# A mixture of experts after attention: a written order for three engines from the first mixture's last two steps on, and a branch put in front of the last stores

## The chip, the cores and the metric

The kernel runs on one core of a Trainium2 chip. The metric is the device time of one launch in microseconds (us), the median of several runs. Each core has five engines that run their own instruction streams in order: TensorE (PE in the rows, with PEld for its weight loads), VectorE (DVE), ScalarE (ACT), GpSimd (POOL) and SyncE (SP). They meet through semaphores only. Here SP issues the loads, and POOL issues the indirect DMAs that scatter rows into a scratch table and the finished rows into the output.

## The reference, cut to what matters

```python
def reference(**kw):                       # q, k, v: 2 x 8 x 768 x 64
    attn = _attn_ref(q, k, v, lam)         # decaying attention, blocks of 64
    x = attn.transpose(0, 2, 1, 3).reshape(1536, 512)
    h = x @ w_in                           # first mixture: 512 -> 2048
    x = (h * np.cos(h)) @ w_out            # 2048 -> 512
    logits = x @ w_gate                    # second mixture: 8 experts
    e_idx = np.argmax(logits, axis=1)
    ...
    for e in range(8):
        mask = e_idx == e
        h = np.maximum(x[mask] @ w1[e], 0.0)      # 512 -> 1024
        out[mask] = gate_w[mask, None] * eom[mask, e, None] * (h @ w2[e])
    return out
```

Each of the 1536 tokens goes to one of eight experts, and its output row is scaled by a softmax weight and a sigmoid of the row itself.

## The kernel before, in words

Matmuls in fp32 precision are made of three fp32r matmuls, with each operand split into a high and a low part: high by high, high by low, low by high. So every weight piece (128 x 1024) is loaded into a `raw` buffer by SP, cast to its high part by ACT and reduced to its low part by DVE; there are five `raw` buffers.

The stages are: attention; the first mixture in steps `B` (256 tokens and a piece of the weights each), whose last three token blocks are finished last (`FIRST`); experts 0 and 1 (`HALVED`) in eight steps `H`, of four tiles of 128 rows in two halves each; experts 2 to 7 in steps `C`, with 208 rows each in two tiles of 104 (`c_first`, `c_second`); then the end.

**The router.** When a block of 256 tokens is finished, `r_tr` transposes it (PE) and copies it to `x2T` (ACT, L582), `r_mm` multiplies by the gates (PE, `lps`, L589), `r_arg` transposes the logits back (PE, `l2ps`, L603) and finds the expert on DVE, and `r_rank` counts the rows of each expert (PE, `rps`, L629 to L632) and scatters the block's rows to the table `xs_d`. After the last block, `routed` issues the loads of the experts' rows from it (`hrows`, L714; `rows`, L736).

**One H step.** `h_l1` multiplies a tile of 128 rows by half of w1 (12 matmuls of 128 x 512 into `hh`, L826) and ACT takes the relu (`hr`, L832). `h_turn` transposes it (4 on PE, `hT`, L838), ACT casts the high part (`hg`, L840) and DVE makes the low part (`hg`, L841). `h_l2` multiplies by half of w2 (12 matmuls into `acc`, L847). `h_prep` and `c_split` transpose rows of x into `xs` (`xps`, L721; ACT L722, DVE L723). `row_scale` works out a row's scale on ACT and DVE (`ng`, L672, first; `who`, L685, last), `finish` scales a tile (`y`, L695 on ACT for the first tile, L697 on DVE for the second) and POOL sends it to the output (L698), one indirect DMA per tile, the "put".

**What orders the work.** Up to step `WHOLE`, the first of experts 2 to 7, the program is written step by step, and the Tile framework's scheduler decides how the instructions follow one another on each engine. From `WHOLE` on, `tc.manual_schedule` fixes PE, DVE and ACT to the written order; SP and POOL are left to the scheduler throughout. After the last step stand a memset of a small tile `warm` on POOL that waits for all puts (L1086), then the load of the count `over` and the branch `tc.If(over > 0)` (L1149). Behind it is a general path for experts that have more rows than their tiles; with these inputs it isn't taken. At last the program's end (L1195), where all engines meet.

```python
    for i in range(NSA + 1, WHOLE):
        step(i)
    phase = tc.manual_schedule(engines={
        mybir.EngineType.PE, mybir.EngineType.DVE, mybir.EngineType.Activation})
    phase.__enter__()
    ends.clear()
    for i in range(WHOLE, len(steps) + LAG):
```

Of the kernel before, what the change touches and what calls it, by code (L numbers as in the profile page):

```python
# [28 lines left out]
def kernel(  # L29
# [130 lines left out]
    order += [(w, e, p) for e in range(HALVED, E) for p in range(EP) for w in ("w1", "w2")]  # L160
# [412 lines left out]
    def r_tr(j):  # L573
# [89 lines left out]
    def row_scale(r, e, n):  # L663
        m = r.shape[0]
        ng = pools["sc"].tile([128, n], F32, tag="ng", name="ng")[0:m]
        ex = pools["sc"].tile([128, n, E], F32, tag="ex", name="ex")[0:m]
        sm = pools["sc"].tile([128, n], F32, tag="sm", name="sm")[0:m]
        ez = pools["sc"].tile([128, n], F32, tag="ez", name="ez")[0:m]
        with ExitStack() as back:
            for ins in ends[-1] if ends else ():  # L670
                back.enter_context(tc.issue_after(ins))
            nc.vector.tensor_scalar(  # L672
                ng.unsqueeze(2), r[:, :, DM + e:DM + e + 1], -1.0, None, ALU.mult)
            for t in range(n):
                nc.scalar.activation(
                    out=ex[:, t, :], in_=r[:, t, DM:DM + E], func=AF.Exp, bias=ng[:, t:t + 1],
                    accum_out=sm[:, t:t + 1])
            nc.scalar.activation(  # L678
                out=ez.unsqueeze(2), in_=r[:, :, DM + E + e:DM + E + e + 1], func=AF.Exp, scale=-1.0)
            nc.vector.tensor_scalar(sm, sm, 1e-9, None, ALU.add)  # L680
# [3 lines left out]
            who = pools["sc"].tile([128, n, 1], I32, tag="who", name="who")[0:m]  # L684
            nc.vector.tensor_copy(out=who, in_=r[:, :, CID:CID + 1].bitcast(I32))  # L685
        return sm, who
# [114 lines left out]

    def c_second(i):
# [12 lines left out]
        if p == EP - 1:  # L815
            acc_t.pop(e)
            s, who = scl.pop(e)
            for z in range(2):
                finish(accs[z], z, s, who[:, z, :])

    def h_l1(e, x, half, turn):
        h = pools["l1"].tile([128, 512], F32, tag="l1", name="hh")
        for z in range(2):
            for kk in range(2):
                for n, (xx, ws) in enumerate(((0, 0), (0, 1), (1, 0))):
                    nc.tensor.matmul(  # L826
                        h, lhsT=x[:, xx, 2 * z + kk, :],
                        rhs=wt["w1", e, 2 * half + z][:, ws, kk * 512:(kk + 1) * 512],
                        start=(z + kk + n == 0), stop=(z == 1 and kk == 1 and n == 2))
            turn()  # L830
        y = tmp_p.tile([128, 512], F32, tag="t", name="hr")
        nc.scalar.activation(out=y, in_=h, func=AF.Relu)  # L832
        return y

    def h_turn(y):
# [6 lines left out]
        return g  # L842

    def h_l2(e, half, g, acc, turn):
        for z in range(4):
            for gs, ws in ((0, 0), (0, 1), (1, 0)):
                nc.tensor.matmul(  # L847
                    acc, lhsT=g[:, gs, z, :], rhs=wB(("w2", e, 2 * half + z // 2), ws, z % 2),
                    start=(half == 0 and z == 0 and gs + ws == 0), stop=(half == 1 and z == 3 and gs == 1))
            if z == 1:  # L850
                turn()
# [9 lines left out]
    def routed():  # L861
# [6 lines left out]
        c_rows(HALVED + 1)  # L868
# [27 lines left out]
    def first(i):  # L896
# [19 lines left out]
        elif ph == "H":  # L916
            y_t[i] = h_l1(j[0], xsp[j], p, turn)
            if j[1] == 1:
                del wt["w1", j[0], 2 * p], wt["w1", j[0], 2 * p + 1]
            if j == (HALVED - 1, 1) and p == 1:  # L920
                for t in range(2):
                    c_split(HALVED, t)
                c_scale(HALVED)

    def second(i):
        ph, j, p = steps[i]
        if p == 0 or (ph == "B" and j < FIRST and p == HP):
            acc_t[j] = [acc_tile([128, DM], "acc") for _ in range(1 if ph == "H" else 2)]
# [18 lines left out]
        elif ph == "H":  # L947
            e, t = j
            h_l2(e, p, g_t.pop(i), accs[0], turn)
            if t == 1:  # L950
                del wt["w2", e, 2 * p], wt["w2", e, 2 * p + 1]
                for _ in range(4 if e == 0 else 0):
                    w_split()
            if p == 1:
                s, who = row_scale(rows.pop(j), e, 1)
                finish(acc_t.pop(j)[0], 0, s, who[:, 0, :])
# [9 lines left out]
    def step(i):  # L966
# [4 lines left out]
        if i == NSB:  # L971
            for _ in range(2):
                second(todo)
                todo += 1
            h_prep(1, 0)
        if i == NSB + 2 * HALVED:
            g_t[i - 1] = h_turn(y_t.pop(i - 1))
            turn()
            h_prep(0, 1)
            for _ in range(2):  # L980
                second(todo)
                todo += 1
                turn()
        if i < len(steps):
            first(i)
        turn()
        if i - 1 in y_t:
            g_t[i - 1] = h_turn(y_t.pop(i - 1))
            turn()
        seconds(max(i - LAG + 1, NSB if i == NSB else 0))  # L990
        if NSB - FIRST * REST <= i < len(steps):
# [4 lines left out]
        if i == NSB + 2 * HALVED:  # L996
            h_prep(1, 1)
# [74 lines left out]
    for i in range(NSA + 1, WHOLE):  # L1072
        step(i)
# [4 lines left out]
    for i in range(WHOLE, len(steps) + LAG):  # L1078
        if i < len(steps):
            c_first(i, i > WHOLE)  # L1080
        if i - 1 in y_t:
            g_t[i - 1] = h_turn(y_t.pop(i - 1))
        (second if i - 2 < WHOLE else c_second)(i - 2)
    phase.__exit__(None, None, None)

    behind(nc.gpsimd.memset(warm, 0.0), puts)  # L1086


    def extra(e, pos):
# [8 lines left out]
        r = pools["rows"].tile([128, 2, ROW], F32, tag="rows", name="xrows")[:, 0:1, :]  # L1098
# [14 lines left out]
        s, _ = row_scale(r, e, 1)  # L1113
# [9 lines left out]
        ps = acc_tile([128, KD, 128], "xps")  # L1123
# [13 lines left out]
        acc = acc_tile([128, DM], "xacc")  # L1137
# [11 lines left out]
    with tc.If(over > 0):  # L1149
# [13 lines left out]
        for e in range(E):  # L1163
# [4 lines left out]
            with tc.For_i(0, n):  # L1168
                extra(e, pos)

# [29 lines left out]
```

## Time and profile before

| | us |
|---|---|
| median of three runs | 532.92 |
| the three runs | 532.25, 532.92, 535.16 |
| the profiled execution, its own time | 535.09 |
| span of its records | 533.3 |
| PE busy in the span | 518.3 (97%) |
| DVE busy | 348.0 (65%) |
| ACT busy | 308.6 (58%) |
| POOL busy | 95.7 (18%) |

The mean granted clock of TensorE in the profiled execution is 0.993 of full speed. The profiled execution is one sample of its own: its time is 2.17 us above the median, and its span begins and ends with the records, 1.8 us short of its time. Busy time of an engine is an average over stages; a stage's own limit is read from what ended the idle time there. A matmul's record includes its way through the pipeline, so records of matmuls that follow one another overlap, and what one costs is the distance between the starts.

### The profile page before, as it was taken

To read this page: it belongs to the slowest core of one execution; us is meant where nothing else is said; L and a number is where in the kernel's file an instruction comes from. 1 tells how busy PE (TensorE), PEld (TensorE's weight loads), DVE (VectorE), ACT (ScalarE), POOL (GpSimd) and SP (SyncE) were. 2 spreads that over 40 slices of the span, in tenths; PEclk is the share of its full clock that TensorE was granted. 3 is DMA by queue.
4 is the path that set the end of the run, shared out by engine and by line. 5 is a ranking of instruction groups with operands and counts; after the bars stand their busy time and mean duration, and the time that the engine had idled before them with its cause. 6 is when DMAs were issued, how large, how long until landed. Compare 5 with 4: busy or idle time off the path is not lost. (4 is left out here: it accounts for less than half of the span.)

```text
span 533.3 us, 9385 instructions
## 1 busy us (share of the span) xinstructions
PE 518.3 (97%) x3644; PEld 454.2 (85%) x3644; DVE 348.0 (65%) x652; ACT 308.6 (58%) x536; POOL 95.7 (18%) x130
## 2 busy tenths in 40 slices
PE   7999999999999999999999999999999999999992
PEld 7889988899898998988888998777888888888881
DVE  5887856887877854454555567932667777777730
ACT  3557655767676765554645576724566656665520
POOL 3455110332222220001021100211010101001011
PEclk9999999999999999999999999999999999999997
DMA  8999941345333392202252256842576778777101
GB/s 201 238 248 266 285 154 41 107 170 198 119 119 119 119 330 77 80 3 80 78 169 97 102 162 199 256 146 92 165 214 209 242 228 247 229 231 215 50 26 36
DMA packets 81939, 84.58 MB, mean 159 GB/s; under 512 B 41468, under 2 KB 61948, under 8 KB 81118
## 3 DMA queue, kind: packets, MB, share of 16 engines
q1 hardware_dynamic: 79646, 77.48, 48.3%
q0 software_dynamic: 2240, 6.42, 3.3%
q8 instruction: 30, 0.49, 0.4%
q14 instruction: 23, 0.19, 0.1%
HBM read 66.70 MB, written 17.65 MB: 158 GB/s over the span
## 5 line engine op out<-in xcount | busy, mean ns | idle before, releaser
L487 PE MATMUL acc<-w_out,g 128*128 128x512 f32 x576 | 140.9, 394 | 0.0
L487 PEld LDWEIGHTS acc<-w_out,g 128*128 128x128 f32 x576 | 104.9, 188 | 22.1 <-issue 1.4
L466 PEld LDWEIGHTS h<-xs,w_in 128*128 128x128 f32 x720 | 88.8, 190 | 2.3 <-DVE a L512 0.5
L466 PE MATMUL h<-xs,w_in 128*128 128x256 f32 x720 | 90.6, 282 | 0.0
L487 PE MATMUL acc<-w_w,g 128*104 128x512 f32 x288 | 70.5, 394 | 0.0
L508 DVE SCALAR_TENSOR_TENSOR a<-a,t 128x512 f32<-128x512 f32 x48 | 36.9, 770 | 44.9 <-ACT a L507 44.9
L487 PEld LDWEIGHTS acc<-w_w,g 128*104 128x104 f32 x288 | 46.7, 168 | 15.4
L476 PE MATMUL hw<-xs,w_w 128*128 128x416 f32 x192 | 59.0, 366 | 0.0
L466 PE MATMUL h<-xback,w_in 128*128 128x256 f32 x432 | 54.9, 282 | 0.0
L466 PEld LDWEIGHTS h<-xback,w_in 128*128 128x128 f32 x432 | 52.8, 189 | 1.4 <-issue 0.8
L506 ACT ACTIVATE t<-h,quarter 128x512 f32<-128x512 f32 x48 | 32.9, 686 | 33.1 <-PE h L466 33.0
L477 PE MATMUL hw<-xs,w_w 128*128 128x208 f32 x192 | 49.3, 257 | 0.0
L772 DVE TENSOR_TENSOR w_w<-raw,w_w 128x1024 fp32r<-128x1024 f32 x40 | 48.6, 1215 | 0.0
L515 ACT CAST g<-a 128x512 fp32r<-128x512 f32 x48 | 29.8, 620 | 30.2 <-DVE a L512 30.2
L512 DVE TENSOR_TENSOR a<-t,h 128x512 f32<-128x512 f32 x48 | 32.9, 685 | 19.6 <-ACT t L511 19.3
L511 ACT ACTIVATE t<-a 128x512 f32<-128x512 f32 x48 | 30.3, 631 | 25.1 <-DVE a L508 25.1
L698 POOL DMA_INDIRECT out_dram<-y,who x16 | 16.4, 1023 | 154.8 <-ACT y L695 122.2
L765 ACT CAST w_w<-raw 128x1024 fp32r<-128x1024 f32 x40 | 42.3, 1057 | 0.0
L516 DVE TENSOR_TENSOR g<-a,g 128x512 fp32r<-128x512 f32 x48 | 33.1, 690 | 12.7 <-ACT g L515 11.9
L783 ACT COPY hsum<-hw 128x208 f32<-128x208 f32 x48 | 15.9, 332 | 41.3 <-PE hw L477 41.3
L477 PEld LDWEIGHTS hw<-xs,w_w 128*128 128x128 f32 x192 | 36.6, 191 | 1.0
L476 PEld LDWEIGHTS hw<-xs,w_w 128*128 128x128 f32 x192 | 36.0, 188 | 1.6
(149 smaller groups left out, 743.0 us busy)
## 6 DMA issues: line engine op xcount, KB each, us to landing
raw<-in_moe_w_dram SPq DMA_DIRECT2D x64, 512.0 KB, 4.4
raw<-in_moe_w_in_dram SPq DMA_DIRECT2D x16, 512.0 KB, 3.8
raw<-in_moe_w_out_dram SPq DMA_DIRECT2D x16, 512.0 KB, 4.4
xs_d<-zrow SPq DMA_DIRECT2D x16, 266.0 KB, 4.4
x_d<-xrow SPq DMA_DIRECT2D x6, 532.0 KB, 3.3
k<-in_k_dram SPq DMA_DIRECT2D x12, 256.0 KB, 3.8
q<-in_q_dram SPq DMA_DIRECT2D x12, 256.0 KB, 5.6
v<-in_v_dram SPq DMA_DIRECT2D x12, 256.0 KB, 5.3
```

Source lines behind the costliest of these rows:

```text
L466: nc.tensor.matmul(h[:, f * n:(f + 1) * n], lhsT=wA(key, ws, kk, f), rhs=x[:, xx, kk, :], start=(z == 0), stop=(z == 3 * KD - 1))
L476: nc.tensor.matmul(h, lhsT=wA(key, 0, kk, f), rhs=x[:, kk], start=(kk == 0), stop=False)
L477: nc.tensor.matmul(h[:, 0, :], lhsT=wA(key, 1, kk, f), rhs=x[:, kk, 0, :], start=False, stop=(kk == KD - 1))
L487: nc.tensor.matmul(accs[t][0:m], lhsT=g[:, gs, f, t * m:(t + 1) * m], rhs=wB(key, ws, f), start=(first and n == 0), stop=(last and n == 5))
L506: head = nc.scalar.activation(out=t, in_=h, func=AF.Identity, bias=quarter, scale=INV2PI / WIDE)
L508: nc.vector.scalar_tensor_tensor(out=a, in0=a, scalar=MAGIC, in1=t, op0=ALU.subtract, op1=ALU.subtract)
L511: nc.scalar.activation(out=t, in_=a, func=AF.Sin, scale=-TWOPI)
L512: nc.vector.tensor_mul(out=a, in0=t, in1=h)
L515: high = nc.scalar.copy(out=g[:, 0].rearrange("p f t -> p (f t)"), in_=a)
L516: low = nc.vector.tensor_sub(out=g[:, 1].rearrange("p f t -> p (f t)"), in0=a, in1=g[:, 0].rearrange("p f t -> p (f t)").bitcast(F32))
L765: nc.scalar.copy(out=t[:, 0, :], in_=r)
L772: nc.vector.tensor_sub(out=t[:, 1, :], in0=r, in1=t[:, 0, :].bitcast(F32))
```

## The change

The manual order now begins with step `NSB`, that is before the last two steps of the first mixture are multiplied by w_out, instead of with `WHOLE`. Between the two, `step`'s loop is replaced by a list that is written out by hand. Within it:

- `h_l1` is called in halves of 6 matmuls, and `h_l2` takes the eight matmuls of the high part of its left operand first and the four of the low part last.
- The casts of the last pieces of experts 0 and 1 are called (`convert_early`) behind the router's steps.
- The scales of the rows (`h_scale`) and the stores (`h_out`) are called apart; `c_scale(2)`, the scale of expert 2's rows, stands behind `h_l2` of the seventh H step.
- `c_rows(3)`, the load of expert 3's rows, is no more in `routed` but behind `h_scale(1, 1)`; expert 2's four pieces of w1 are loaded ahead of its four of w2.

At the end, the memset of `warm` is gone, and `c_store(7)`, the scaling and the two puts of the last expert, stands behind the `If`. The general path takes its working tiles from other pools; it isn't run.

```diff
@@
-    order += [(w, e, p) for e in range(HALVED, E) for p in range(EP) for w in ("w1", "w2")]
+    order += [(w, HALVED, p) for w in ("w1", "w2") for p in range(EP)]
+    order += [(w, e, p) for e in range(HALVED + 1, E) for p in range(EP) for w in ("w1", "w2")]
...
+    def c_store(e, accs):
+        s, who = scl.pop(e)
+        for z in range(2):
+            finish(accs[z], z, s, who[:, z, :])
...
-            for z in range(2):
-                finish(accs[z], z, s, who[:, z, :])
...
+            if e < E - 1:
+                c_store(e, accs)
+            else:
+                acc_t["last"] = accs
...
-        for z in range(4):
-            for gs, ws in ((0, 0), (0, 1), (1, 0)):
...
+        for n, (gs, z, ws) in enumerate([(0, z, ws) for z in range(4) for ws in range(2)] + [(1, z, 0) for z in range(4)]):
...
         h_rows(1)
         c_rows(HALVED)
-        c_rows(HALVED + 1)
...
-            if j == (HALVED - 1, 1) and p == 1:
-                for t in range(2):
-                    c_split(HALVED, t)
-                c_scale(HALVED)
...
-    for i in range(NSA + 1, WHOLE):
+    for i in range(NSA + 1, NSB):
         step(i)
...
+    second(NSB - 2)
+    h_l1(H, 0)
+    second(NSB - 1)
+    rout.clear()
+    h_l1(H, 1)
+    r_tr(last, (0,))
+    r_tr(last, (1,))
+    h_l1(H + 1, 0)
+    h_prep(1, 0)
+    r_mm(last)
+    h_turn(H)
+    h_l1(H + 1, 1)
+    r_arg(last)
+    h_l1(H + 2, 0)
+    r_rank(last)
+    convert_early(1)
+    h_l1(H + 2, 1)
+    h_turn(H + 1)
+    routed()
+    h_l2(H)
+    convert_early(1)
+    h_l1(H + 3, 0)
+    h_l1(H + 3, 1)
+    h_turn(H + 2)
+    convert_early(2 * EP * HALVED)
+    h_scale(0, 0)
+    h_l2(H + 1)
+    h_out(0, 0)
+    h_turn(H + 3)
+    h_l2(H + 2)
+    h_prep(0, 1)
+    h_scale(1, 0)
...
+    h_turn(H + 4)
+    h_scale(0, 1)
+    h_scale(1, 1)
+    c_rows(HALVED + 1)
+    c_split(HALVED, 0)
+    h_l1(H + 6, 0)
+    h_l1(H + 6, 1)
+    h_turn(H + 5)
+    c_split(HALVED, 1)
+    convert(2)
+    h_l2(H + 4)
+    h_l1(H + 7, 0)
+    h_l1(H + 7, 1)
+    h_turn(H + 6)
+    convert(2)
+    h_l2(H + 5)
+    h_out(0, 1)
+    convert(2)
+    c_first(WHOLE, True)
+    h_turn(H + 7)
+    h_l2(H + 6)
+    c_scale(HALVED)
+    c_first(WHOLE + 1, True)
+    h_l2(H + 7)
+    h_out(1, 1)
+    for i in range(WHOLE + 2, len(steps) + LAG):
...
-    behind(nc.gpsimd.memset(warm, 0.0), puts)
...
             with tc.For_i(0, n):
                 extra(e, pos)
+    c_store(E - 1, acc_t["last"])
```

How the rows of three engines move. In these listings a row is a line of the kernel, the operation and its tiles; `w_w_1_2` is piece 2 of expert 1 (its last two numbers apart), and the line numbers of the changed kernel are its own.

ACT, from the last cosine step of the first mixture to the last router block, before:

```order
L511 ACTIVATE t<-a 128x512
L202 CAST w_w_1_2_4084<-raw 128x1024
L515 CAST g<-a 128x512
L722 CAST xs<-xps 128x4x128
L678 ACT_TABLE_LOAD
L678 ACTIVATE ez<-hrows 128x1 x2
L675 ACTIVATE ex,sm<-hrows,ng 128x8 x2
L202 CAST w_w_1_3_4174<-raw 128x1024
L582 COPY x2T<-x2ps 128x512 x2
```

and now:

```order
L512 ACTIVATE t<-a 128x512
L516 CAST g<-a 128x512
L849 ACTIVATE hr<-hh 128x512
L583 COPY x2T<-x2ps 128x4x128 x2
L726 CAST xs<-xps 128x4x128
L857 CAST hg<-hT 128x512
L849 ACTIVATE hr<-hh 128x512
L769 CAST w_w_1_2_4154<-raw 128x1024
```

The casts of pieces 2 and 3 of expert 1, which stood in front of the copies to `x2T`, stand behind them.

DVE, behind the totals of the router, before:

```order
L643 TENSOR_TENSOR si<-sl,ov 128x2
L841 TENSOR_TENSOR hg<-hT,hg 128x512
L858 TENSOR_SCALAR more<-more 128x8
L859 TENSOR_REDUCE most<-more 128x1
L841 TENSOR_TENSOR hg<-hT,hg 128x512
L672 TENSOR_SCALAR ng<-rows 104x2
L672 TENSOR_SCALAR ng<-hrows 128x1
L841 TENSOR_TENSOR hg<-hT,hg 128x512
```

and now:

```order
L887 TENSOR_REDUCE most<-more 128x1
L776 TENSOR_TENSOR w_w_1_3_4210<-raw,w_w_1_3_4210 128x1024
L858 TENSOR_TENSOR hg<-hT,hg 128x512
L677 TENSOR_SCALAR ng<-hrows 128x1
L685 TENSOR_SCALAR sm<-sm 128x1
L686 TENSOR_SCALAR ez<-ez 128x1
L687 TENSOR_TENSOR sm<-sm,ez 128x1
L688 RECIPROCAL sm<-sm 128x1
L689 COPY who<-hrows 128x1
L858 TENSOR_TENSOR hg<-hT,hg 128x512
```

The first step of expert 2's scale (`ng` from `rows`, 104x2) stood in front of an `hg`; it is no more in this stretch.

SP, from the loads of the experts' rows on, before:

```order
L714 DMA hrows<-xs_d 128x532 x2
L736 DMA rows<-xs_d 104x2x532
L184 DMA raw<-in_moe_w_dram 128x4x256
L184 DMA raw<-in_moe_w_dram 128x2x512
L184 DMA raw<-in_moe_w_dram 128x4x256 x2
L184 DMA raw<-in_moe_w_dram 128x2x512
L736 DMA rows<-xs_d 104x2x532
```

and now:

```order
L718 DMA hrows<-xs_d 128x532 x2
L740 DMA rows<-xs_d 104x2x532
L185 DMA raw<-in_moe_w_dram 128x2x512
L740 DMA rows<-xs_d 104x2x532
L185 DMA raw<-in_moe_w_dram 128x2x512 x3
L185 DMA raw<-in_moe_w_dram 128x4x256
```

The second load of `rows` (expert 3's) stands behind one load of a weight piece instead of five.

## Rows read from the trace of the kernel before

**Rows 1.** Busy time by stretch: from, to, length; busy us of PE, PEld, DVE, ACT, POOL.

```profile
339.00:404.00 65.00, 62.95 (x335) 51.85 (x333) 33.77 (x88) 34.16 (x67) 8.68 (x8) 1.00 0.54 169
```

**Rows 2.** Timeline at the last router block, PE and ACT: start, us, what, [idle before].

```profile
344.89 1.18 PE L826 MATMUL hh<-w_w,xs 128*128 128x512 f32 x4
346.63 0.64 PE L589 MATMUL lps<-x2T,wgs 128*32 128x256 f32 x8 [0.55 <-ACT x2T L582]
...
344.56 1.05 ACT L202 CAST w_w<-raw 128x1024 fp32r<-128x1024 f32 x1 [1.23 <-DMA raw<-in_moe_w_dram]
```

**Rows 3.** Timeline of PE and DVE in the second layer of experts 0 and 1.

```profile
363.74 0.71 PE L847 MATMUL acc<-w_w,hg 128*128 128x512 f32 x2
365.64 5.28 PE L847 MATMUL acc<-w_w,hg 128*128 128x512 f32 x22 [1.19 <-DVE hg L841]
...
364.77 0.17 DVE L672 TENSOR_SCALAR ng<-rows 104x2 f32<-104x2 f32 x1 [8.91 <-DMA rows<-xs_d]
```

**Rows 4.** Timeline of PE and SP's queue where expert 2 begins.

```profile
389.82 0.35 PE L476 MATMUL hw<-xs,w_w 128*128 128x416 f32 x1
...
392.69 0.55 PE L721 MATMUL xps<-ident,rows 104*128 104x104 f32 x4 [0.30 <-DMA rows<-xs_d]
...
386.82 0.34 SPq L736 DMA_DIRECT2D rows<-xs_d  x1
```

**Rows 5.** Timeline of PE at the last block's logits and ranks.

```profile
348.00 0.38 PE L603 MATMUL l2ps<-ident,lt 128*128 128x128 f32 x2
...
350.30 0.18 PE L629 MATMUL rps<-ohb,upper 128*128 128x8 bf16 x1
```

**Rows 6.** Timeline of the last 18 us, all engines.

```profile
515.43 8.46 PE L487 MATMUL acc<-w_w,g 128*104 128x512 f32 x36
...
521.21 0.69 ACT L695 ACTIVATE y<-acc,sm 104x512 f32<-104x512 f32 x1 [4.26 <-PE acc L487]
522.19 0.99 POOL L698 DMA_INDIRECT out_dram<-y,who  x1 [12.06 <-ACT y L695]
523.93 0.75 DVE L697 TENSOR_SCALAR y<-acc,sm 104x512 f32<-104x512 f32 x1 [6.36 <-PE acc L487]
524.98 1.00 POOL L698 DMA_INDIRECT out_dram<-y,who  x1 [1.79 <-DVE y L697]
529.94 0.10 POOL L1086 MEMSET warm<- 128x1 f32 x1 [3.96 <-DMA out_dram<-y,who]
```

**Rows 7.** The branch's line: sequencer operations, ns min/median/max, first to last start.

```profile
L1149 POOLq EVENT_SEMAPHORE  x6: 17/30/43, 528.3 to 528.7; - x6
...
L1149 ACTq EVENT_SEMAPHORE  x2: 17/17/17, 524.3 to 524.4; - x2
L1149 DVEq EVENT_SEMAPHORE  x2: 21/21/21, 527.9 to 528.0; - x2
...
L1149 ACTq COMPARE_BRANCH  x1: 50/50/50, 521.8 to 521.8; - x1
L1149 DVEq COMPARE_BRANCH  x1: 72/72/72, 524.6 to 524.6; - x1
L1149 POOLq COMPARE_BRANCH  x1: 53/53/53, 525.3 to 525.3; - x1
```

**Rows 8.** The line of the program's end, the same columns.

```profile
L1195 SPq EVENT_SEMAPHORE  x14: 17/28/28, 529.5 to 533.2; - x14
...
L1195 POOLq DRAIN  x3: 40/113/2488, 529.9 to 533.0; - x3
L1195 SPq DRAIN  x3: 7/7/7, 530.2 to 532.7; - x3
```

**Rows 9.** DMA issues from 520 to 533: count, median us to landing.

```profile
out_dram<-y,who POOLq DMA_INDIRECT x2, 3.4
```

**Rows 10.** A weight piece's way from the page; ACT's casts where expert 2 begins.

```profile
raw<-in_moe_w_dram SPq DMA_DIRECT2D x64, 512.0 KB, 4.4
...
387.92 3.15 ACT L202 CAST w_w<-raw 128x1024 fp32r<-128x1024 f32 x3
```

More of the change, by code (lines that the diff above doesn't have):

```diff
@@ L577, in r_tr @@
         x2T = lps_t["x2T"]
-        for t in range(2):
+        for t in tiles:
             ps = acc_tile([128, KD, 128], "x2ps")
@@ L816, in c_second, with h_l1, h_turn @@
             acc_t.pop(e)
-            s, who = scl.pop(e)
-            for z in range(2):
-                finish(accs[z], z, s, who[:, z, :])
[L821 to L835, printed above, removed]
+            if e < E - 1:
+                c_store(e, accs)
+            else:
+                acc_t["last"] = accs
+    hh_t = {}
+    def h_l1(i, z):
+        _, (e, t), half = steps[i]
+        x = xsp[e, t]
+        if z == 0:
+            hh_t[i] = pools["l1"].tile([128, 512], F32, tag="l1", name="hh")
+        h = hh_t[i]
+        for kk in range(2):
+            for n, (xx, ws) in enumerate(((0, 0), (0, 1), (1, 0))):
+                nc.tensor.matmul(
+                    h, lhsT=x[:, xx, 2 * z + kk, :],
+                    rhs=wt["w1", e, 2 * half + z][:, ws, kk * 512:(kk + 1) * 512],
+                    start=(z + kk + n == 0), stop=(z == 1 and kk == 1 and n == 2))
+        if t == 1:
+            del wt["w1", e, 2 * half + z]
+        if z == 1:
+            y_t[i] = tmp_p.tile([128, 512], F32, tag="t", name="hr")
+            nc.scalar.activation(out=y_t[i], in_=hh_t.pop(i), func=AF.Relu)
+    def h_turn(i):
+        y = y_t.pop(i)
         ps = acc_tile([128, 4, 128], "hT")
@@ L841, in h_turn, with h_l2, h_scale, h_out @@
         nc.vector.tensor_sub(out=g[:, 1], in0=ps, in1=g[:, 0].bitcast(F32))
-        return g
-    def h_l2(e, half, g, acc, turn):
-        for z in range(4):
-            for gs, ws in ((0, 0), (0, 1), (1, 0)):
[L847 to L851, printed above, removed]
+        g_t[i] = g
+    def h_l2(i):
+        _, (e, t), half = steps[i]
+        g = g_t.pop(i)
+        if half == 0:
+            acc_t[e, t] = acc_tile([128, DM], "acc")
+        acc = acc_t[e, t]
+        for n, (gs, z, ws) in enumerate([(0, z, ws) for z in range(4) for ws in range(2)] + [(1, z, 0) for z in range(4)]):
+            nc.tensor.matmul(
+                acc, lhsT=g[:, gs, z, :], rhs=wB(("w2", e, 2 * half + z // 2), ws, z % 2),
+                start=(half == 0 and n == 0), stop=(half == 1 and n == 11))
+        if t == 1:
+            del wt["w2", e, 2 * half], wt["w2", e, 2 * half + 1]
+    def h_scale(e, t):
+        scl[e, t] = row_scale(rows.pop((e, t)), e, 1)
+    def h_out(e, t):
+        s, who = scl.pop((e, t))
+        finish(acc_t.pop((e, t)), 0, s, who[:, 0, :])
     def totals():
@@ L946, in second @@
                 del wt["out", p]
[L947 to L956, printed above, removed]
     todo = 0
@@ L970, in step @@
             h_prep(0, 0)
[L971 to L985, printed above, removed]
-        turn()
[L987 to L991, printed above, removed]
+        first(i)
+        turn()
+        seconds(i - LAG + 1)
+        if NSB - FIRST * REST <= i:
             n = 0
@@ L1077, with convert, convert_early @@
     ends.clear()
-    for i in range(WHOLE, len(steps) + LAG):
+    heads.clear()
+    assert not rout and todo == NSB - 2
+    H, last = NSB, FIRST - 1
+    def convert(n=1):
+        for _ in range(n):
+            c_high()
+            c_low()
+    def convert_early(n):
+        for _ in range(n):
+            if nxt["split"] < wide + 2 * EP * HALVED:
+                convert()
+    second(NSB - 2)
[30 more added lines that the diff above has]
+    h_scale(1, 0)
+    h_l2(H + 3)
+    h_out(1, 0)
+    h_l1(H + 4, 0)
+    h_l1(H + 4, 1)
+    h_prep(1, 1)
+    h_l1(H + 5, 0)
+    h_l1(H + 5, 1)
+    h_turn(H + 4)
[24 more added lines that the diff above has]
+    for i in range(WHOLE + 2, len(steps) + LAG):
         if i < len(steps):
[L1080 to L1083, printed above, removed]
+            c_first(i, True)
+        c_second(i - 2)
     phase.__exit__(None, None, None)
-    behind(nc.gpsimd.memset(warm, 0.0), puts)
     def extra(e, pos):
@@ L1097, in extra @@
         who = pools["xt1"].tile([128, 1], I32, tag="who", name="who")
-        r = pools["rows"].tile([128, 2, ROW], F32, tag="rows", name="xrows")[:, 0:1, :]
+        r = pools["rows"].tile([128, 2, ROW], F32, tag="rows", name="xrows")
+        r, spare = r[:, 0:1, :], r[:, 1, :]
         nc.gpsimd.indirect_dma_start(
```

31 lines of the change are left out of this document (13 added, 18 removed).

## The prediction, made before the changed kernel was run

> **What bounds the kernel now.** First the page's busy times, in the table above: PE is busy for 97% of the span, and the change removes no matmul, so only the time in which PE stands still, and what follows its last matmul, can be gained. Then busy time by stretch: from 339 to 404 us, which holds most of the stages that get the written order, PE is busy 62.95 of 65.00 us [rows 1]. So 2.05 us of idle time is all that those records show. Third, the timelines, for what ended each pause; there are three, of 0.55, 1.19 and 0.30 us, 2.04 together [rows 2 to 4]. Since records of matmuls overlap, I price a pause by the distance between starts, less what the work in it costs. Matmuls of 128x512 that wait for nothing cost 0.235 us each (36 in 8.46 [rows 6]), or 0.24 (22 in 5.28 [rows 3]). Last, the end: PE's last matmul ends at 515.43 + 8.46 = 523.89 [rows 6], and the span ends at 533.3. So 9.4 us lie behind the bound, in which only ACT, DVE, POOL, DMA and the branch work.
>
> **The pause in front of the last router block.** PE starts four matmuls at 344.89 and the router's `lps` at 346.63: 1.74 us for four times 0.238, so 0.79 lost. The row puts it down to ACT's `x2T`; ACT itself had stood 1.23 us for a weight piece's DMA, cast it at 344.56 for 1.05, and only then copied `x2T` [rows 2]. In the changed order that cast stands behind the copies, and PE has six matmuls and four transposes between x2T's transposes and `lps`. Two copies have that long. I take all 0.79 as gained. The piece that is cast later is of w2 of expert 1, used only in the second layer, which PE reached at 363 to 371 [rows 3].
>
> **The pause in front of expert 1's second layer.** Two matmuls start at 363.74, the next 22 at 365.64: 1.90 less 0.47, so 1.43 lost to DVE's `hg`. DVE had stood 8.91 us for expert 2's rows and began `ng` of them at 364.77, one place ahead of that `hg` [rows 3]. With `c_scale(2)` moved behind the seventh H step's second layer, nothing in DVE's stretch waits for that DMA; the scale that now stands there reads `hrows`, block 0's rows, which came long before. All 1.43 are gained.
>
> **The pause where expert 2 begins.** From 389.82 to 392.69 are 2.87 us in which PE does 16 matmuls that cost 2.40 by the starts of their eight pairs (0.30 a pair). So 0.47 are lost to the rows of expert 2 or 3, whose load was issued at 386.82 behind five weight pieces [rows 4]. Now it stands behind one piece and waits for its buffer, which `h_scale(1, 1)` gives back, by my placing of that step between 381 and 385. That is 2 to 6 us earlier, against 0.47 lost. All of it is gained: 0.79 + 1.43 + 0.47 = 2.69 for the three, where idle records alone give 2.04.
>
> **What the new order adds.** Between `l2ps` and `rps`, DVE finds the experts of the last block. The two start 2.30 us apart, under nine matmuls of 0.238 and l2ps's own 0.14, which fill it [rows 5]. The list puts only one `h_l1` call of six there: 1.43 + 0.14 = 1.57. So PE may wait 2.30 - 1.57 = 0.73 us. What that chain of DVE steps needs by itself is not shown, since PE was in time; it is between nothing and 2.30, and I take the upper end, because `rps` followed its matmuls without a gap to spare. The count of rows (`cps`) now waits for the last DVE addition of the rank step, which I set at one small DVE step, 0.14 (by the 0.17 of `ng` [rows 3], mostly covered by the matmuls ahead). Together 0.87. The order of terms within `h_l2` changes no count; it gives DVE's low part eight matmuls, 1.9 us, more time. That is cover and no gain of its own. The stage thus gains 2.69 - 0.87 = **1.82**, at most 2.69.
>
> **The end.** Behind the last matmuls ACT scales one tile at 521.21, DVE the other at 523.93, and POOL issues the last put from 524.98 to 525.98 [rows 6]. Then the three branch: ACT at 521.8 with its next row at 524.3, DVE at 524.6 with 527.9, POOL at 525.3 with 528.3, so 2.5, 3.3 and 3.0 us [rows 7]. After that POOL's memset begins at 529.94, and the row puts its wait down to the puts [rows 6]. But the last put lands some 3.4 us after its issue [rows 9], at 528.4, so the memset stood for POOL's own way through the branch. The end is entered at 529.5 by SP and 529.9 by POOL, whose DRAIN takes 2.49, to 532.4; then 0.9 to the end of the span [rows 8].
>
> With the branch in front of the last tiles, ACT takes it behind its last `g`, with 4.26 us of idle time ahead of its `y`, DVE with 6.36 [rows 6]: both cover the 2.5 and 3.3. POOL takes it after expert 6's puts, ahead of 12.06 us of idle time [rows 6]. PE takes it after its last matmul, as now. So the way through the branch is hidden, and the memset's 0.10 goes. POOL's DRAIN can begin at 525.98 and ends at 528.5, about when the put lands. Then SP's walk over its semaphores, 529.5 to 530.2, so 0.7, and the 0.9 of the close [rows 8]: 528.4 + 0.7 + 0.9 = 530.0 against 533.3. The gain is **3.3**. Its bounds: 3.9, if only the DRAIN stands in the way (528.5 + 0.9 = 529.4), and 1.5, if the DRAIN begins when the put has landed (rival one).
>
> The price of the branch decides here, and the rows show it as 2.5 to 3.3 us on each engine [rows 7]. The Trainium skill, "Runtime: NRT & Kernel Launch", section "Instruction fetch mechanics", says that a taken branch whose target lies outside the fetched window makes the engine fetch it before it goes on; the trace agrees with a wait of that kind, and by that rule the jump to the program's end could be a second one (rival three).
>
> **The sum.** 1.82 + 3.3 = 5.1 us. Against the profiled execution that is 535.09 - 5.1 = 530.0. That execution is 2.17 above the median of the runs shown, which are 2.9 apart, so I take the sum off the median: 532.92 - 5.1 = **527.8**. A measurement of this kernel can tell about 0.5%, 2.7 us, from no change, which puts the bound for faster at 530.3.
>
> **Rivals.**
> One: the DRAIN on POOL begins only after the last put has landed, as it did before (529.9, when all was landed). Then 528.4 + 2.49 + 0.9 = 531.8, a gain at the end of 1.5, in all 3.3: **529.6**. For it: DRAIN's 2.49 in the only case shown, and that nothing tells what it waits for. Against it: it took that long with no transfer left. Chance 0.12.
>
> Two: the order only moves the pauses. What PE waits for is late again elsewhere (the rank chain at its full length, a cast that now stands in front of a relu), and the H stretch gains nothing: 532.92 - 3.3 = **529.6**. For it: idle time is only 3% of that stretch [rows 1], and ACT and DVE are each busy over half of it, so an order without pauses is tight. Against it: each of the three waits is for one instruction that the listings show moved. Chance 0.08.
>
> Three: the way through the branch comes back at another jump, on POOL between the last put and the end: 525.98 + 3.0, then the DRAIN's 2.49 and 0.9 make 532.4, a gain of 0.9; in all 2.7, so **530.2**. For it: the code of the end lies behind the general path, and POOL jumps to it. Against it: the present kernel has such a jump behind the memset, and the DRAIN begins in the same tenth of a microsecond as the memset [rows 6, 8]. Chance 0.06.
>
> Four, to the slow side: SP's queue. The load of expert 3's rows now stands in front of seven weight pieces, and until `h_scale(1, 1)` has freed its buffer nothing passes it. The sixth piece of expert 2 lands 4.4 us after its issue [rows 10], so at 385.8 to 389.8 if the rows are issued at 381 to 385. ACT's third cast in the present run begins at about 390.0 [rows 10], which is where the new list has the sixth piece. The margin is 0 to 4 us, and PE has work beyond it for about 5 (a second layer of 12 matmuls, 2.86, and an expert's first layer, 2.40). In a written order ACT stands at that cast with a relu and an `hg` behind it, and PE stops. It decides from some 7 us of delay on. At 10 us PE loses 3 if that cover holds and 10 if it doesn't, with the H stretch's gain gone: 532.92 - 3.3 + 3 = 532.6 to 539.6, in the middle **536.1**. For it: the order of SP's queue, which had sent five pieces ahead of that load and now sends one. Against it: the buffer is freed by steps that PE's own progress brings. Chance 0.04.
>
> **How the numbers follow.** 0.70 is left for the forecast. It holds 526.3 (2.69 + 3.9 gained) to about 529; rivals one to three lie at 529.6 to 530.2, and runs of one kernel scatter by one or two us. The range 526.0 to 530.8 takes them in and leaves out rival four and some scatter. Faster by over 0.5%: the forecast, one and two, 0.90, less 0.07 for measured times that fall beyond 530.3, so 0.83. Within: three and that scatter, 0.13. Slower: rival four, 0.04.
>
> **What would show it.** In the profile of the changed kernel: no pause of PE in front of `lps`, at expert 1's second layer, or in front of expert 2's `xps`; a new one of up to 0.73 in front of `rps`; PE busy for all but about 1 us of the same 65. At the end: the branch's rows on ACT, DVE and POOL ahead of their last tile's rows, POOL's DRAIN right behind the last put, and about 6 us from PE's last matmul to the end of the span instead of 9.4. It is wrong if those 6 stay above 8 (three), if the DRAIN starts after the landing (one), if PE's idle time in the stretch stays at 2 (two), or if PE stops where expert 2 begins (four).

## The result, and the profile after

| | before | after |
|---|---|---|
| median of six runs, us | 534.43 | 528.96 |
| lowest and highest | 532.25, 535.74 | 528.00, 529.86 |
| ratio, 95% interval | | 0.9906 [0.9888, 0.9923] |
| the profiled execution | 535.09 | 529.07 |
| its span | 533.3 | 527.3 |

The change makes the kernel 5.0 us faster by the ratio (0.0094 x 534.43; 4.1 to 6.0 by its interval). The forecast was a sum of 5.1 and a time of 527.8 in a range of 526.0 to 530.8. The sum is what was measured; the time came out 1.2 higher because the kernel before has a median of 534.43 in six runs, 1.5 above that of the three that the forecast started from.

The span on the page of the kernel after, and then busy time in the stretch of [rows 1]:

```profile
span 527.3 us, 9379 instructions
```

```profile
339.00:404.00 65.00, 64.75 (x346) 53.93 (x346) 36.51 (x91) 36.30 (x71) 7.86 (x8) 1.00 0.55 176
```

PE now idles 0.25 us of those 65 instead of 2.05. All of it is one pause, ahead of the ranks. PE's timeline from x2T's transposes to the ranks, after:

```profile
344.00 1.04 PE L582 MATMUL x2ps<-ident,xrow 128*128 128x128 f32 x8
344.79 1.64 PE L841 MATMUL hh<-w_w,xs 128*128 128x512 f32 x6
346.27 0.60 PE L725 MATMUL xps<-ident,hrows 128*128 128x128 f32 x4
346.80 0.64 PE L590 MATMUL lps<-x2T,wgs 128*32 128x256 f32 x8
347.37 0.66 PE L855 MATMUL hT<-ident,hr 128*128 128x128 f32 x4
347.78 1.64 PE L841 MATMUL hh<-w_w,xs 128*128 128x512 f32 x6
349.25 0.38 PE L604 MATMUL l2ps<-ident,lt 128*128 128x128 f32 x2
349.39 1.62 PE L841 MATMUL hh<-w_w,xs 128*128 128x512 f32 x6
351.26 0.18 PE L630 MATMUL rps<-ohb,upper 128*128 128x8 bf16 x1 [0.25 <-DVE ohb L619]
```

`lps` follows without a bracket, where [rows 2] had 0.55. From `l2ps` to `rps` are 2.01 us for matmuls that cost 1.57, so PE loses 0.44 there (0.25 by the records). The 2.01 are the length of DVE's chain, and the trace before has it too: there `l2ps` starts at 348.00 [rows 5], and the chain's last step, which `rps` reads, ends at 349.95, 1.95 later:

```profile
349.78 0.17 DVE L618 CAST ohb<-oh 128x16 bf16<-128x16 f32 x1
```

The end, after: the timeline, the branch's line and the line of the program's end.

```profile
518.43 0.69 ACT L699 ACTIVATE y<-acc,sm 104x512 f32<-104x512 f32 x1 [4.26 <-PE acc L488]
519.42 1.00 POOL L702 DMA_INDIRECT out_dram<-y,who  x1 [12.06 <-ACT y L699]
521.16 0.75 DVE L701 TENSOR_SCALAR y<-acc,sm 104x512 f32<-104x512 f32 x1 [6.36 <-PE acc L488]
522.20 1.00 POOL L702 DMA_INDIRECT out_dram<-y,who  x1 [1.78 <-DVE y L701]
```

```profile
L1214 POOLq EVENT_SEMAPHORE  x6: 17/30/43, 509.5 to 509.9; - x6
L1214 ACTq EVENT_SEMAPHORE  x2: 17/17/17, 516.6 to 516.7; - x2
L1214 DVEq EVENT_SEMAPHORE  x2: 21/21/21, 517.7 to 517.8; - x2
...
L1214 POOLq COMPARE_BRANCH  x1: 53/53/53, 506.7 to 506.7; - x1
...
L1214 ACTq COMPARE_BRANCH  x1: 50/50/50, 514.2 to 514.2; - x1
L1214 DVEq COMPARE_BRANCH  x1: 72/72/72, 514.8 to 514.8; - x1
```

```profile
L1261 SPq EVENT_SEMAPHORE  x14: 17/28/14610, 510.7 to 527.2; - x14
...
L1261 POOLq DRAIN  x3: 40/113/4506, 522.0 to 527.0; - x3
L1261 SPq DRAIN  x3: 7/7/7, 526.0 to 526.7; - x3
```

The way through the branch is about as long as it was (POOL 506.7 to 509.5, ACT 514.2 to 516.6, DVE 514.8 to 517.7, against [rows 7]), but each engine has passed it before its last tile comes. The last put now starts at 522.20 and ends at 523.20, and the span ends 4.1 us later; before, it ended at 525.98, 7.3 us ahead of the end [rows 6].

**Where the time went.** Four starts in PE's timeline cut an execution into stages: the first w_in matmul of the first mixture, its last one, the first w2 matmul of expert 2, and the last matmul of all. Between the second and the third lies the written order; behind the fourth, the end. In each trace, in us (variants without a ratio were run once):

| kernel | to first w_in | w_in | written order | experts 2 to 7 | end | ratio to before |
|---|---|---|---|---|---|---|
| before | 37.88 | 295.17 | 71.11 | 119.34 | 9.76 | |
| after | 37.36 | 295.19 | 68.79 | 119.37 | 6.59 | 0.9906 |
| tail_only | 36.40 | 295.31 | 71.07 | 119.34 | 6.60 | 0.9935 |
| order_only | 37.95 | 295.35 | 68.69 | 119.37 | 9.81 | 0.9972 |
| no_memset | 36.93 | 295.18 | 71.07 | 119.34 | 9.28 | 0.9997 |
| memset_back | 36.47 | 295.28 | 69.08 | 119.37 | 7.94 | 0.9936 |
| cast_front | 36.30 | 295.30 | 68.76 | 119.37 | 6.55 | |
| scale_front | 37.23 | 295.17 | 70.42 | 119.37 | 6.57 | |
| l2_terms | 37.85 | 295.36 | 68.68 | 119.37 | 6.58 | |
| rows_late | 36.28 | 295.23 | 74.24 | 119.37 | 6.59 | |
| b_scale | 36.50 | 295.22 | 69.22 | 119.34 | 9.89 | |
| scale_l2 | 37.05 | 295.24 | 73.80 | 119.37 | 6.59 | |
| best | 37.36 | 295.14 | 68.52 | 119.37 | 6.82 | 0.9895 |
| rank_cover | 36.84 | 295.14 | 68.69 | 119.37 | 6.54 | 0.9903 |

The spans differ by 6.0 us: 2.32 in the written order, 3.17 at the end, and 0.52 ahead of the first w_in matmul, in attention, which the change doesn't touch. That first stage spreads over 1.7 us between executions, the others agree within 0.2 where the program is the same (the written order of `memset_back`, with a pause of 0.19 of its own, within 0.4). So a stage's own length tells tenths where whole times tell whole microseconds.

### The profile page after: what moved, and what is told of

It is laid out like the page before. It is cut to its first block, busy times and chain, and to the rows that moved or that the text cites. A ratio compares the mean times of both kernels' runs of the same rounds, so it can differ in the third digit from the quotient of the medians.

```text
span 527.3 us, 9379 instructions
## 1 busy us (share of the span) xinstructions
PE 517.1 (98%) x3644; PEld 454.7 (86%) x3644; DVE 348.2 (66%) x652; ACT 308.7 (59%) x536; POOL 93.9 (18%) x129
## 5 line engine op out<-in xcount | busy, mean ns | idle before, releaser
L776 DVE TENSOR_TENSOR w_w<-raw,w_w 128x1024 fp32r<-128x1024 f32 x50 | 60.6, 1216 | 0.8 <-ACT w_w L769 0.8
L769 ACT CAST w_w<-raw 128x1024 fp32r<-128x1024 f32 x50 | 52.5, 1056 | 0.0
```

The lines of the kernel that those rows point to most:

```text
L769: nc.scalar.copy(out=t[:, 0, :], in_=r)
L776: nc.vector.tensor_sub(out=t[:, 1, :], in0=r, in1=t[:, 0, :].bitcast(F32))
```

## Experiments

### The two parts apart

The kernel before with the new end (`tail_only`), and the changed kernel with the old one (`order_only`):

```diff
@@ tail_only, in the kernel before
+            if e < E - 1:
+                c_store(e, accs)
+            else:
+                acc_t["last"] = accs
...
-    behind(nc.gpsimd.memset(warm, 0.0), puts)
...
+    c_store(E - 1, acc_t["last"])
@@ order_only, in the changed kernel
-            if e < E - 1:
-                c_store(e, accs)
-            else:
-                acc_t["last"] = accs
+            c_store(e, accs)
...
+    behind(nc.gpsimd.memset(warm, 0.0), puts)
...
-    c_store(E - 1, acc_t["last"])
```

> The kernel before with the new end alone (branch in front of the last tiles, no memset); the order of the stages ahead is as it was. Theory (the two parts add up, and the end is worth what it showed in the changed kernel): PE's pauses of 0.55, 1.19 and 0.30 us stay, and from PE's last matmul to the end of the span there are 6.2 us instead of 9.4, so 3.2 us less, ratio 0.994. Rival (the end only gains beside the new order): under 1 us.

> The changed kernel with the old end (the last tiles' stores and the memset in front of the branch). Theory: PE's last matmul comes 2.7 us earlier than in the kernel before, 9.4 us follow it as before, ratio 0.995. Rival (what the order gains is given back at the end): under 1 us.

`tail_only`: 530.01 against 533.68, ratio 0.9935 [0.9915, 0.9954], which is 2.5 to 4.5 us; by stage 3.16, with the three old pauses by the records (0.41, 1.08, 0.57). `order_only`: 532.14, ratio 0.9972 [0.9961, 0.9984], 0.9 to 2.1 us; by stage 2.42. The end's gain needs no new order, and the order's gain isn't given back at the end. The two ratios add up to 5.0 us, the whole. Why the times of `order_only` show 1.5 us (0.0028 x 533.68) where its stage shows 2.4 isn't settled; the first stage, which each trace samples once, is the only other one that varies.

### What held the end: the branch or the wait for the puts

```diff
@@ no_memset, in the kernel before
-    behind(nc.gpsimd.memset(warm, 0.0), puts)
@@ memset_back, in the changed kernel
     c_store(E - 1, acc_t["last"])
+    behind(nc.gpsimd.memset(warm, 0.0), puts)
```

> The kernel before without the memset that waits for all puts, the branch where it was. Theory (POOL's way through the branch, not the wait for the puts, held the end): from PE's last matmul to the end of the span 9.0 to 9.4 us, so 0 to 0.4 us less, ratio 0.999 to 1. Rival (the memset's 3.96 us of waiting are the cost): 2.5 to 3.3 us less, ratio 0.995.

> The changed kernel with the memset, which waits for all puts, put back at its very end. It tells what POOL's last DRAIN waits for. Theory (the DRAIN takes about 2.5 us by itself, and is partly hidden under the last put's way): landing at 3.4 us after the put's issue, 0.1 for the memset, 2.5 for the DRAIN, 0.8 to close, so 7.9 us from PE's last matmul to the end instead of 6.2, 1.7 us more than the changed kernel, ratio to before 0.994. Rival (the DRAIN waits for the landing anyway, and is short behind it): 0 to 0.3 us more than the changed kernel.

`no_memset`: ratio 0.9997 [0.9982, 1.0013], the end 9.28 instead of 9.76. The memset's 3.96 us of waiting [rows 6] cost at most half a microsecond: POOL was in the branch meanwhile. `memset_back`: 530.03, ratio 0.9936 [0.9921, 0.9952], the end 1.35 us longer than after. POOL's last two rows in its trace, and the DRAIN of the program's end:

```profile
521.69 1.00 POOL L702 DMA_INDIRECT out_dram<-y,who  x1 [1.78 <-DVE y L701]
524.81 0.10 POOL L1236 MEMSET warm<- 128x1 f32 x1 [2.12 <-DMA out_dram<-y,who]
```

```profile
L1262 POOLq DRAIN  x3: 40/113/2498, 524.8 to 527.9; - x3
```

The put has landed 3.1 us after its start, and a DRAIN that starts behind the landing still takes 2.50. So the landing isn't what its time is spent on. In the changed kernel its record starts at 522.0, ahead of the put, and ends at 526.5, 3.3 us after the put's end, while SP's walk, which had waited 14.6 us from 510.7 for the landing at 525.3, is through at 526.0. The DRAIN is the last link, by half a microsecond. Rival one of the prediction would have had the end of `memset_back`.

### One thing of the order, in the kernel before

```diff
@@ b_scale: expert 2's scale behind the last hg called ahead of it, on DVE
-                c_scale(HALVED)
+                with tc.issue_after(g_t["low"].ins):
+                    c_scale(HALVED)
```

> The kernel before with one thing of the change alone: the scale of expert 2's rows is queued on DVE behind the last hg that is called ahead of it, so no hg stands behind the wait for those rows. The stretch from the first mixture's last w_in matmul to expert 2's first w2 matmul is 71.11 us in the kernel before and 71.07 in two others with its order. Theory (the three pauses are not three independent terms: the one at lps was covered by the one at hg, which ended when the rows landed; with that one gone the one at lps counts): the pause at expert 1's second layer is gone, the stretch is 69.3 to 69.8 us. Second theory (three independent terms): 1.43 less, 69.7, with pauses at lps and expert 2's xps as before; the two are told apart by a run in which the pause at lps is short. Rival (what is gained comes back whole at the next wait): 70.8 or more.

The stretch is 69.22, 1.89 less, by this one step. PE in `b_scale`, at `lps`, in the second layer of expert 1 and where expert 2 begins, and the load of expert 3's rows:

```profile
345.22 0.64 PE L589 MATMUL lps<-x2T,wgs 128*32 128x256 f32 x8 [0.47 <-ACT x2T L582]
```

```profile
362.32 3.90 PE L847 MATMUL acc<-w_w,hg 128*128 128x512 f32 x16
```

```profile
383.02 0.88 PE L721 MATMUL xps<-ident,rows 104*128 104x104 f32 x8
...
389.47 0.55 PE L721 MATMUL xps<-ident,rows 104*128 104x104 f32 x4
```

```profile
383.93 0.34 SPq L736 DMA_DIRECT2D rows<-xs_d  x1
```

The pause ahead of `hg` is gone, the one at `lps` stays, and the one at expert 2's `xps` has gone as well, by landing: PE needed those rows 5.5 us after their issue and had them. In the kernel before they took 5.9 (392.69 - 386.82 [rows 4]) and in `tail_only` 6.1; why they were faster in this one execution isn't shown. Neither theory held whole, as the stretch is below the 69.3 of the first and the 69.7 of the second. What was measured is two of the prediction's terms: 71.11 - 1.43 - 0.47 = 69.21.

The first theory needs the pause at `lps` to be covered by the one at `hg`. The execution of `no_memset` seems to say so: it has no pause at `lps`, the same 71.07, and at `hg`

```profile
364.75 5.28 PE L847 MATMUL acc<-w_w,hg 128*128 128x512 f32 x22 [1.72 <-DVE hg L841]
```

1.72 where [rows 3] has 1.19. But the loads of expert 2's rows went out earlier there too, counted from the start of the written order by 0.48 us, as much as `lps` came earlier. What took longer was the load. Its issue before, and its issue and first reading in `no_memset`:

```profile
359.61 0.45 SPq L736 DMA_DIRECT2D rows<-xs_d  x1
```

```profile
358.19 0.45 SPq L736 DMA_DIRECT2D rows<-xs_d  x1
```

```profile
363.88 0.17 DVE L672 TENSOR_SCALAR ng<-rows 104x2 f32<-104x2 f32 x1 [9.43 <-DMA rows<-xs_d]
```

That is 5.16 us before (364.77 [rows 3]), 5.69 in `no_memset` and 5.61 in `tail_only` (363.16 - 357.55), with the same order up to there. A load that differs by half a microsecond between executions can hide a pause of that size, so these traces don't tell whether the pause at `lps` was worth something by itself. No run takes it away alone.

**The buffer, not the queue.** In the kernel before, expert 3's rows are issued 0.2 us after the eight transposes of expert 2's rows end, which are 0.72 long by the starts: 383.02 + 0.72 = 383.74 and 383.93 here, 385.91 + 0.72 = 386.63 and 386.82 in the trace before ([rows 4]; the transposes' row is the first below). There are two such buffers. The other one, with the rows of the second tiles, was read until 402.4 before, and until 378.9 after:

```profile
385.91 0.88 PE L721 MATMUL xps<-ident,rows 104*128 104x104 f32 x8
```

```profile
L685 DVE COPY who<-hrows x2: 133/144/154, 374.6 to 402.4; 128x1 int32<-128x1 int32 x2
```

```profile
L689 DVE COPY who<-hrows x4: 134/134/135, 362.5 to 378.9; 128x1 int32<-128x1 int32 x4
```

```profile
379.19 0.32 SPq L740 DMA_DIRECT2D rows<-xs_d  x1
```

So it is `h_scale(1, 1)`, now some 23 us earlier, that lets the load go.

### Taking single steps back in the changed kernel

```diff
@@ cast_front
+    c_high()
     r_tr(last, (0,))
...
     r_rank(last)
-    convert_early(1)
+    c_low()
@@ scale_front
     h_out(0, 0)
+    nc.vector.tensor_scalar(warm[0:HL, :], rows[HALVED, 2][:, 0, DM + HALVED:DM + HALVED + 1], -1.0, None, ALU.mult)
     h_turn(H + 3)
@@ l2_terms (scale_l2 has this and scale_front)
-        for n, (gs, z, ws) in enumerate([(0, z, ws) for z in range(4) for ws in range(2)] + [(1, z, 0) for z in range(4)]):
+        for n, (gs, z, ws) in enumerate([(gs, z, ws) for z in range(4) for gs, ws in ((0, 0), (0, 1), (1, 0))]):
@@ rows_late
-    c_rows(HALVED + 1)
     c_split(HALVED, 0)
...
     c_split(HALVED, 1)
     convert(2)
+    with tc.issue_after(raw_t["load"].ins):
+        c_rows(HALVED + 1)
```

> The changed kernel with one cast (the high part of piece 2 of expert 1's w2, on ACT) put back in front of the copies to x2T; its low part on DVE stays where it is. Read from the trace: PE's distance from x2T's transposes to lps, 2.80 us in the changed kernel, and the pause ahead of lps, 0 there. Theory (ACT is in order, so the copies wait for the cast, and that for its piece): 0.1 to 0.4 us of pause if the piece has landed when ACT comes to it, since six matmuls and four transposes now stand in between and give about 1 us, and one for one more for each us that the piece lands later. Rival (the cover alone cured this pause): none.

No pause at `lps`, and 68.76. ACT and PE in `cast_front`:

```profile
343.73 1.03 ACT L769 CAST w_w<-raw 128x1024 fp32r<-128x1024 f32 x1
344.66 1.07 ACT L583 COPY x2T<-x2ps 128x512 f32<-128x512 f32 x2
```

```profile
345.82 0.64 PE L590 MATMUL lps<-x2T,wgs 128*32 128x256 f32 x8
```

The cast stands in front of the copies again, but its piece is there, and the copies end at 345.7, just in time for `lps`. So the six matmuls and four transposes in between suffice to cover a cast of 1.03 us, as the rival said. But the run puts back the cast of piece 2. The one that stood directly in front of the copies in the kernel before was piece 3's, and it had first stood 1.23 us for its DMA [rows 2]. Here the copies end 0.1 us ahead of `lps`, so a wait of that kind would hardly have been covered; no run tries it.

> The changed kernel with one small DVE step that reads expert 2's rows (one column of them, into a spare tile) put in front of the low part of hg of the fourth H step. Theory (DVE stands at that step until the rows have landed, some 5.2 us after their issue at 362.3, and hg, queued behind, is late): DVE waits to about 367.4, hg's low part comes at about 368.2, and PE, which needs it after eight of the twelve matmuls that start at 365.65, so at 367.55, pauses 0.5 to 1.0 us. Rival (the pause before was the term order of h_l2, not the DVE step): no pause.

> The small DVE step that reads expert 2's rows in front of hg, as in scale_front, and the old order of terms in h_l2. Theory (the term order is cover: hg's low part is needed after two matmuls instead of eight, six times 0.238 earlier): the pause of 1.46 us grows to 2.9, and the stretch from 70.42 to 71.8. Rival (the term order covers nothing): 1.5 us of pause as before.

In `scale_front` DVE stood 5.78 us, the rows landed 6.3 us after their issue at 361.86, where I had expected 5.2, and PE paused 1.46. DVE and PE there, and PE in `scale_l2`:

```profile
368.15 0.15 DVE L1110 TENSOR_SCALAR warm<-rows 104x1 f32<-104x1 f32 x1 [5.78 <-DMA rows<-xs_d]
```

```profile
368.95 1.20 PE L868 MATMUL acc<-w_w,hg 128*128 128x512 f32 x4 [1.46 <-DVE hg L858]
```

```profile
369.21 3.88 PE L868 MATMUL acc<-w_w,hg 128*128 128x512 f32 x10 [3.24 <-DVE hg L858]
```

One DVE step that reads late rows in front of `hg` brings the pause back, so that mechanism is shown. With the old term order the pause is 3.24 (2.9 expected, and the rows came 0.35 us later in this run), so the cover of six matmuls is worth about their own time, 1.4 us. The stretch grew by more than the pause did, 3.38 against 1.78; see the last section.

> The changed kernel with the old order of terms in h_l2 (the low part of the left operand as every third matmul, so first needed after two matmuls instead of eight). Theory (cover and no gain of its own: DVE's low part is ready before its matmuls start): the stretch from the first mixture's last w_in matmul to expert 2's first w2 matmul within 0.3 us of the changed kernel's 68.80. Rival (the terms' order is what took the pause ahead of expert 1's second layer away): 1 to 1.5 us more, with a pause put down to DVE's hg.

68.68, and no pause but the one at `rps`: the term order alone is cover and no gain, as forecast.

> The changed kernel with the load of expert 3's rows queued on SP behind three more weight pieces (four instead of one). Theory (the rows take 5.9 us from issue to PE, as they did before, and SP's queue sets the issue): issued at about 388 instead of 379.2, so PE's transposes of expert 3's rows, at 389.9 in the changed kernel, stand 3 to 5 us. Rival (the pause before was the rows' own way or DMA load, not their place in the queue): under 1 us.

SP's load and PE's transposes in `rows_late`:

```profile
387.22 0.38 SPq L740 DMA_DIRECT2D rows<-xs_d  x1
```

```profile
392.71 0.58 PE L725 MATMUL xps<-ident,rows 104*128 104x104 f32 x4 [3.76 <-DMA rows<-xs_d]
```

Behind three more pieces the rows go out 9.1 us later, counted from the start of the written order in each trace, PE stands 3.76 us, and the stretch is 74.24. So the queue's order does count once the buffer is early.

### Towards a faster one

```diff
@@ rank_cover and best, with h_turn cut into its transposes and its copies
+    h_turn_pe(H + 1)
     r_rank(last)
...
     h_turn(H + 1)
@@ best alone, for the very last tile
+            nc.scalar.activation(out=y[:, 0:256], in_=acc[:, 0:256], func=AF.Copy, scale=s[:, t:t + 1])
+            nc.vector.tensor_scalar(y[:, 256:DM], acc[:, 256:DM], s[:, t:t + 1], None, ALU.mult)
```

> The changed kernel with two additions: the four transposes of the second H step stand between l2ps and rps on PE (their copies on ACT and DVE stay where they were), and the very last tile is scaled in two halves by ACT and DVE at once instead of by DVE alone. Theory: the transposes, 0.36 us, cover the remaining pause of 0.25 at rps, so the stretch goes from 68.79 to about 68.5; the half of a 0.75 us step saves 0.3 us at the end, 6.59 to 6.3 from PE's last matmul's start to the end of the span; 0.6 us less than the changed kernel in all, ratio to before about 0.989. Rival (the ranks or the rows come later for it, and PE waits for them at the first layer of the second tiles): the stretch stays at 68.8 or grows, and only the end gains.

> The changed kernel with only the four transposes of the second H step moved between l2ps and rps on PE, the last tile scaled by DVE alone as in the changed kernel. Theory: the stretch from the last w_in matmul to expert 2's first w2 matmul is 68.5 us, as with both additions, instead of 68.79, and the end 6.59 as in the changed kernel, so 0.27 us less, ratio to before 0.990. Rival (the halves of the last tile were not what lengthened the end by 0.23): the end stays at 6.8.

`best`: 528.40, ratio 0.9895 [0.9879, 0.9912]; `rank_cover`: 528.35, ratio 0.9903 [0.9877, 0.9928]. Neither can be told from the change's 0.9906. In both, no pause of PE is left in the stretch (68.52 and 68.69, where the same order with the pause gave 68.68 to 68.79), so by the stretch what the pause of 0.25 was worth isn't settled beyond 0 to 0.3 us. Counted from the start of `lps` alone, traces agree better: 54.53 to 54.55 us in the changed kernel and four variants that keep the pause (`order_only`, `memset_back`, `cast_front`, `l2_terms`), 54.38 and 54.41 in these two. So it was worth some 0.15 us. The halves of the last tile cost 0.23 at the end instead of saving 0.3. ACT and DVE in `best`:

```profile
520.83 0.47 ACT L699 ACTIVATE y<-acc,sm 104x256 f32<-104x256 f32 x1 [2.03 <-PE acc L488]
```

```profile
521.34 0.48 DVE L700 TENSOR_SCALAR y<-acc,sm 104x256 f32<-104x256 f32 x1 [6.86 <-ACT y L699]
```

They didn't run at once: DVE was released by ACT, and two halves of 0.47 in a row are longer than one whole of 0.75. Both read one accumulator and write one tile `y`. The Trainium skill, "PSUM — Partial Sum Buffer", section "PSUM bank collisions raise a hardware error", says that two engines must not access the same bank and quadrant at once, reads included, and that the compiler's scheduler puts a dependency between them; the order in this trace agrees, though it doesn't tell the accumulator from the shared `y` as its reason.

## Why the prediction was right, point by point

**What bounds it.** Right. The stages ahead and behind, 295.2 and 119.4 us, are the same to 0.2, and only PE's pauses and the end moved.

**The written order: 1.82 forecast, at most 2.69; 2.32 measured.** The mechanism held and two terms were mis-sized. The rank chain's wait, put at 0.73, is 0.44 by the starts, since DVE's chain needs 2.01 us and not 2.30. The prediction said that the chain's own length is not shown; the trace before shows it (348.00 to 349.95), and a wait of about 0.4 could have been forecast from it. The count's wait for DVE, put at 0.14, shows as no pause. With 2.69 for the three pauses this gives 2.25.

**The three pauses as three terms.** The sum came out, and so did two terms together: the move of expert 2's scale alone gave 1.89 (`b_scale`), with 1.43 + 0.47 = 1.90 in the prediction for the two pauses that went. That the 0.47 went with it is in part luck, a load that was faster in that execution. The term at `lps`, 0.79, is not shown by itself. By the idle records alone the stretch would have gained 2.04 - 0.25 = 1.79; the distances between starts were the better price.

**Why the pause at `lps` went.** The prediction gave the cast's place as the reason and the six matmuls as cover. `cast_front` shows that the cover is enough for a cast whose piece has landed; for one that still waits, as in the kernel before, which of the two was needed stays open.

**Why the pause where expert 2 begins went.** The prediction read "issued behind five weight pieces" from SP's listing. What held the load was its buffer, as the 0.2 us behind the transposes show in two traces; the pieces only stood ahead of it. The step it named for the change, `h_scale(1, 1)` giving a buffer back, is the right one, at 379 instead of 381 to 385.

**The end: 3.3 forecast, 3.17 measured.** The branch is hidden on all engines, as forecast, and the memset's wait was covered by it (`no_memset`). From the put's end to the span's end 4.0 us were forecast (525.98 to 530.0) and 4.1 measured. But the last link is POOL's DRAIN, not the landing and SP's walk, which end 0.5 us earlier. That the two agree to 0.1 is luck: the DRAIN ended 3.3 us behind the put where 2.5 was forecast, and the landing came after 3.1 instead of 3.4. Why this DRAIN ends 0.8 later than its 2.5 isn't shown.

**The rivals.** One: a DRAIN that starts behind the landing costs 1.35 us (`memset_back`), and it doesn't start there. Two: the pauses did not move elsewhere. Three: no second way through a branch shows on POOL, whose DRAIN follows the put. Its premise, a wait at a taken branch, stays: 2.4 to 2.9 us on these engines, 2.5 to 3.3 before, but hidden now. Four: expert 3's rows went out at 379.2, before any delay could build up; `rows_late`, which delays the rows and not the pieces, shows what one late load costs in a written order, 5.45 us.

## What to carry to other kernels

Price a pause of the bounding engine by the distance between starts less what the work in it costs, not by the idle record, and look in the same trace for the length of the chain that will be waited for next. A gain of a few tenths that hangs on when a load lands can't be read from one execution. When a load is late, look at who last read its buffer before blaming the queue it stands in. Work that every engine must pass once, such as a branch around code that isn't run, belongs where each engine waits anyway, ahead of the last tile instead of behind it.

## What the runs showed of the hardware that was not expected

**TensorE's clock falls after a longer pause.** In `scale_front` PE stood 1.46 us, and the granted clock stayed at 1.00, the level of 2.4 GHz. In `scale_l2` it stood 3.24, in `rows_late` 3.76, and in both the clock then fell to 0.50, the level of 1.2 GHz, with PE busy again. Busy time by stretch in `scale_l2` (the granted clock is the third number from the end):

```profile
370.00:371.00 1.00, 1.00 (x4) 0.79 (x3) 0.62 (x5) 0.33 (x3) 0.00 (x0) 0.56 0.00 0
371.00:372.00 1.00, 1.00 (x3) 0.75 (x3) 0.00 (x0) 0.00 (x0) 0.00 (x0) 0.50 0.00 0
372.00:373.00 1.00, 1.00 (x4) 0.77 (x3) 0.00 (x0) 0.00 (x0) 0.00 (x0) 0.50 0.00 0
373.00:374.00 1.00, 1.00 (x5) 0.82 (x4) 0.00 (x0) 0.69 (x1) 0.00 (x0) 0.73 0.00 0
```

and in `rows_late`:

```profile
393.00:394.00 1.00, 1.00 (x8) 1.00 (x7) 0.14 (x1) 0.51 (x1) 0.00 (x0) 0.55 1.06 390
394.00:395.00 1.00, 1.00 (x4) 0.81 (x4) 0.60 (x2) 0.59 (x1) 0.00 (x0) 0.50 1.03 388
395.00:396.00 1.00, 1.00 (x3) 0.78 (x3) 0.62 (x2) 0.30 (x2) 0.00 (x0) 0.50 1.08 392
396.00:397.00 1.00, 1.00 (x5) 0.74 (x4) 0.52 (x5) 0.47 (x5) 0.00 (x0) 0.75 1.00 375
```

The missing clock adds up to 1.7 us in either (0.44 + 0.50 + 0.50 + 0.27, and 0.45 + 0.50 + 0.50 + 0.25), and so the stretch grew by 5.45 in `rows_late` for a pause of 3.76, and in `scale_l2` by 3.38 for 1.78 more of pause. Behind the 1.72 us of `no_memset` the granted clock stayed at 1.00. Each of these is one execution, and no run has a pause between 1.72 and 3.24. The prediction's rival four, priced by the pause alone, was too cheap by such an amount.

**POOL's DRAIN** at the program's end takes 2.35 to 2.50 us when nothing is left to land (in `no_memset` 2353 ns, in `memset_back` 2498 ns), and ends 3.3 us after an indirect put when it is queued right behind it.

```profile
L1194 POOLq DRAIN  x3: 40/107/2353, 528.6 to 531.5; - x3
```
